# Chunked attention and a Fourier mixing block on one core: the first batch's fold halves joined in PSUM, sines ahead of the exponentials, Pool work re-ranked

## The chip, the cores and the metric

One NeuronCore of a Trainium2 chip runs the kernel. The metric is the device time of one execution in microseconds; below it is written "us". The engines are TensorE (PE, with PEld for its weight loads), VectorE (DVE), ScalarE (ACT), GpSimd (POOL) and SyncE (SP, which only issues transfers here).

## The reference, cut to what matters

There are 4 batches, 8 heads, 768 positions and 64 numbers per head. Each chunk of 32 positions attends to 8 memory keys and to its context of 16 positions to the left, itself and 8 to the right. The heads' outputs side by side are `x` (768 x 512 per batch).

```python
for c in range(24):
    k_full = concat([mem_k, k[l_start:r_end]]); v_full = concat([mem_v, v[l_start:r_end]])
    a = softmax(q_c @ k_full.T / 8)
    x[c] = a @ v_full
u = x + real(fft(fft(x, axis=1), axis=2))        # over positions, then over the 512 columns
un = (u - mean(u)) / sqrt(var(u) + 1e-6)
out = u + relu(un @ w_ch1) @ w_ch2               # 512 -> 2048 -> 512
```

## The kernel before, in words

The kernel has three parts per batch: attention for four pairs of heads, the Fourier step, and an MLP. It builds a list of tasks with an engine, a cost, predecessors, buffers that are taken and given, and a rank. `Plan.order` (L54) runs a clock over these costs and writes down the tasks in the order in which they would start; each engine then gets its instructions in this order and works through them strictly in it. The plan's clock sets only the order. On the chip an instruction waits by a semaphore for those that share data or a buffer with it, and for nothing else.

**Attention** (`attention`, L654; pair number `n` 0 to 3 is the first batch). SP loads `q` and `k` in float32 (`qf`, `kf`, three buffers each) and `v` with a column of ones (`va`, three buffers). The queries and keys are cast to bfloat16 (`e_cast_q` L293, `e_cast_k` L297), on DVE for the first batch and on POOL for the others; POOL also copies the part of `va` that overlaps the next chunk (`e_overlap` L301). TensorE transposes both (`trq`, `trk`), ACT evicts them (`qT` L314, `kTb` L335), and for each half `g` of the sequence TensorE makes scores (`sc` L346, one buffer), ACT the exponential (`e` L354), TensorE the product with the values (`xa` L367, one PSUM buffer), and DVE divides by the sum into `xsb` (L377, L378). Scores need the copy of the memory keys into `kTb` (L330).

**Fourier, later batches** (`part_of_later` L780). The columns and positions are folded on DVE (`zy`, `pq`, `ff`), so that cosines and sines act on half the length. Each folded tile is split into a float16 part `hi` (ACT, L425) and the remainder `lo` (DVE, L430). TensorE multiplies both with the tables `cosS`, `sinS` along positions (`ps`, L440: the row products), `up` holds the result as two float16 parts again (L452 on ACT, L456 on DVE), `dn` is its reversal (L461), and TensorE multiplies with the tables `cosD`, `nsinD`, `sinD` along columns (`pm`, L472).

**Fourier, first batch** (`part_of_first` L808). The folding is done by halves `h` of the column range, so that the half of pairs 0 and 1 (heads 0, 1, 6, 7) can start before pairs 2 and 3 are there: `pq` L482 and L483, `ff` L497 to L500. Each half has its own row products, cosine and sine, and its own `up`; one edge column gets twelve products with one column of weights (`e0_edge`, L509). The columns step then adds up eight products for each of the two parities of the output column, those of the second half with the tables `tab1` that POOL makes from `alt` (L739, L740): 16 products for each of six tiles, 96 in all (`pm` L531).

**Tail of a Fourier step**: for each of six tiles `kt`, DVE adds `pm` to `xsb` (L538), makes mean and variance (L544, L545), ACT subtracts the mean (`un` L550), TensorE transposes (`tp` L557), and DVE evicts into `unT` (L562). POOL makes `rstd` (L566).

**MLP** (`mlp` L882): `ph` (L578, 64 matmuls per half batch), relu on ACT (`hT` L585), `pc` (L592, 48), then `osb` on DVE (L598) and the store. POOL issues the loads of both weights, which are cast to float16 on the way: `w1` (L770) behind the last overlap copy of the first batch, `w2` (L775) behind those of the second pair of the second batch.

**The tables**: DVE makes angles in three steps (L636, L639, L641) and their absolute value (L644) for positions (`S`) and columns (`D`); the sines are one ACT task (`e_all_sines`, seven activations, L719 to L724) that depends on the last exponential of the first batch:

```python
t_sines = add("ACT", 6.2, e_all_sines, [t_angle["S"], t_angle["D"], x_last])
```

POOL then turns `tab1` and writes the tables' first rows (L747 to L752). Where no other task of TensorE is ready, the plan puts groups of six products with zeros (`warm` L390).

Of the kernel before, what the change touches and what calls it, by code (L numbers as in the profile page):

```python
# [12 lines left out]
FP16 = mybir.dt.float16  # L13
AFT = mybir.ActivationFunctionType
# [20 lines left out]
class Plan:  # L35
# [18 lines left out]
    def order(self):  # L54
        now, idle, wire = 0.0, {}, 0.0
# [8 lines left out]
        while any(waiting.values()):  # L64
# [4 lines left out]
            for e, ts_ in waiting.items():  # L69
                if idle.get(e, 0.0) > now:  # L70
                    continue
                for t in ts_:
# [17 lines left out]
                    if t["moved"]:  # L90
                        wire = max(wire, now + cost) + t["moved"]
                        t["done"] = t["end"] = wire + self.LAG["DMA"]
                    else:
                        t["done"] = now + cost + self.LAG.get(e, 0.07)
# [20 lines left out]
def kernel(  # L115
# [40 lines left out]
    NS = 3  # L156
    qf = [spool.tile([QP, 2, RB * D], FP32, name=f"qf{i}") for i in range(NS)]
# [6 lines left out]
    HP = H // 2  # L164
# [21 lines left out]
    svD = cpool.tile([P, 1], FP32)  # L186
    zero = cpool.tile([P, 1], FP32)
# [15 lines left out]
    tab1_of = []  # L203
    alt = wpool.tile([P, 2, HD], FP16)
    c384 = cpool.tile([P, NST], FP32)
    e256 = cpool.tile([P, 2, NST], FP16)
    w1_sb = wpool.tile([P, NDT, DFF], FP16)
    w2_sb = wpool.tile([P, NHT, DM], FP16)

    def e_zero():  # L210
        nc.vector.memset(zeros, 0.0)
        nc.vector.memset(zero, 0.0)  # L212
        nc.vector.memset(hpi_b, math.pi / 2.0)
        nc.vector.memset(mhalf, -0.5)

# [39 lines left out]
    def e_mkf():  # L255
        for par in range(2):
            nc.scalar.dma_start(mkf[:, par], bass.AP(
                tensor=mem_k.tensor, offset=mem_k.offset + par * NMEM * D,
                ap=[[2 * NMEM * D, NPR], [D, NMEM], [1, D]]))
# [12 lines left out]
    def e_load_v(n, hh):  # L272
        b, pr = seq[n]
        v1 = va[n % NV]
# [26 lines left out]
    def e_overlap(n, hh):  # L301
        v1 = va[n % NV][:, hh]
# [47 lines left out]
    def e_exp(n, g):  # L350
        sc = sc_of.pop((n, g))
        e1_of[n, g] = e1 = apool.tile([P, 2, 6, 64], FP32, tag="e1", bufs=3, name="e1")
# [5 lines left out]
    def e_values(n, g):  # L358
        e1 = e1_of.pop((n, g))
        xa = aps.tile([P, 3, 2, 66], FP32, tag="xa", bufs=1, name="xa")  # L360
        xa_of[n, g] = xa
        for st in range(3):
            for hh in range(2):
                v1 = va[n % NV][:, hh]
# [17 lines left out]

    warm_of = []
# [10 lines left out]
    mu_of, unT_of, rstd_of = {}, {}, {}  # L394

# [24 lines left out]
    def e_hi(b, par, ab):  # L420
        if ab == 0:
# [10 lines left out]

    def e_rows(b, par, ab):
        ps_of[b, par, ab] = ps = fps.tile([P, 2, NK], FP32, tag="acc", name="ps")

        def dft(out_, tab, c0, c1):
            for sp in range(2):
                for st in range(3):
                    for i, part in enumerate(hl_of[b, par]):
                        nc.tensor.matmul(out_[:, sp, :], part[:, ab, sp * 3 + st, c0:c1],  # L440
                                         tab[:, sp, st, :], start=(st == 0 and i == 0),
                                         stop=(st == 2 and i == 1))

        dft(ps, cosS if ab == 0 else sinS, 0, P)
        if par == 0 and ab == 1 and b > 0:
            dft(ps[0:1], cosS, 0, 1)
# [29 lines left out]

    def e0_pq(h, i):
# [8 lines left out]
        elif i == 1:  # L486
            nc.vector.tensor_copy(e256[:, 0], pq[:, :, P])
            nc.vector.tensor_tensor(e256[:, 1], pq[:, :, P], e256[:, 0], ALU.subtract)

    def e0_ff(h, ab):  # L490
# [4 lines left out]
        op = ALU.add if ab == 0 else ALU.subtract  # L495
        if h == 0:
            nc.vector.tensor_copy(ff[:, ab, :, 0], pq[:, :, 0])  # L497
        else:
            nc.vector.tensor_tensor(ff[:, ab, :, 0], pq[:, :, 0], c384, op)
        nc.vector.tensor_tensor(ff[:, ab, :, 1:P], pq[:, :, 1:P],  # L500
                                rev_ap(pq, HD - 1, P - 1, [[HD, NST]]), op)

    def e0_edge():

        ps_of["edge"] = ps = fps.tile([P, 2, NK], FP32, tag="acc", name="ps")
        for sp in range(2):
            for st in range(3):
                for i in range(2):
                    nc.tensor.matmul(ps[0:1, sp, :], e256[:, i, sp * 3 + st:sp * 3 + st + 1],  # L509
                                     cosS[:, sp, st, :], start=(st == 0 and i == 0),  # L510
                                     stop=(st == 2 and i == 1))

    def e0_edge_up(part):
        up = up_of[0, 0, 1][2][0:1]
        if part == 0:
            nc.scalar.copy(up[:, 0].rearrange("p k s -> p s k"), ps_of["edge"][0:1])
        else:
            nc.vector.tensor_tensor(up[:, 1].rearrange("p k s -> p s k"), ps_of.pop("edge")[0:1],
                                    up[:, 0].rearrange("p k s -> p s k"), ALU.subtract)

    def e0_columns(kt):
        pm_of[0, kt] = pm = fps.tile([P, 2, HD], FP32, tag="acc", name="pm")
        tab1 = tab1_of[0]
        for par in range(2):
            im = 0
            for h in range(2):
                for ab in range(2):
                    i = 0 if ab == 0 else (1 if kt < 3 else 2)
                    rhs = (cosD, nsinD, sinD)[i] if h == 0 else tab1[:, i]
                    for part in range(2):  # L530
                        nc.tensor.matmul(pm[:, par, :],  # L531
                                         up_of[0, h, ab][kt // 3][:, part, ts(kt % 3, P)],
                                         rhs[:, par, :], start=(im == 0), stop=(im == 7))
                        im += 1
# [12 lines left out]
    def e_un(b, kt):  # L547
        un_of[b, kt] = un = fpool.tile([P, DM], FP16, tag="un", bufs=3, name="un")

        nc.scalar.activation(un, xs[b][:, kt, :], AFT.Identity, bias=mu_of[b][:, kt, 0:1],  # L550
                             scale=-1.0)

    def e_turn_u(b, kt):
        un = un_of.pop((b, kt))
        tp_of[b, kt] = tp = fps.tile([P, NDT, P], FP16, tag="acc", name="tp")
# [3 lines left out]
    def e_unT(b, kt):  # L559
        if kt == 0:  # L560
            unT_of[b] = fpool.tile([P, NDT, S], FP16, tag="unT", bufs=2, name="unT")
        nc.vector.tensor_copy(unT_of[b][:, :, ts(kt, P)], tp_of.pop((b, kt)))  # L562
# [44 lines left out]
    t_mkf = add("ACT", 0.2, e_mkf, moved=0.8)  # L607
# [3 lines left out]
    t_clear["va", 0, 0] = add("ACT", 1.0, lambda: e_clear_act(va[0][:, 0]), [t_zero])  # L611
    t_clear["va", 0, 1] = add("POOL", 0.9, lambda: nc.gpsimd.memset(va[0][:, 1], 0.0))
    t_scales = add("DVE", 0.2, e_scales, [t_iota])
    t_idb = add("DVE", 0.25, lambda: nc.vector.tensor_copy(ident_b, ident), [t_id])
    t_masks = add("POOL", 0.9, e_masks)
    for i in range(1, NS):
        t_clear["kf", i] = add("ACT", 1.15, lambda i=i: e_clear_act(kf[i]), [t_zero])
        for hh in range(2):
            t_clear["va", i, hh] = add("ACT", 1.0, lambda i=i, hh=hh: e_clear_act(va[i][:, hh]),
                                       [t_zero])  # L620
    for i in range(NKT):
        t_clear["kTb", i] = add("POOL", 0.5, lambda i=i: nc.gpsimd.memset(
            kTb[i].rearrange("p (b c) -> p b c", b=NB)[:, :, 64:96], 0.0))
    t_col = add("DVE", 0.6, e_rows_of_ones, [t_id])
    t_ones = {i: add("DVE", 0.1, lambda i=i: e_ones(i),
                     [t_col, t_clear["va", i, 0], t_clear["va", i, 1]]) for i in range(NV)}
# [6 lines left out]
    for nm, parts, y, r, NN, c in (("S", tabS, yS.rearrange(fl3), rS.rearrange(fl3), S, 1.3),  # L633
# [328 lines left out]
```

## Time and profile before

| what | value |
|---|---|
| time, median of 7 runs | 319.54 us (317.72 to 323.25) |
| the profiled execution | 319.59 us, of which the span from first to last instruction is 317.8 us |
| mean granted TensorE clock | 0.984 of full speed |
| busy: PE, DVE, ACT, POOL | 295.2, 191.4, 167.9, 88.8 us |
| first exponential; last one of the first batch | starts 11.40; ends 32.7 us |
| the seven sines and their table load | 32.72 to 38.3 us |
| first product of the columns step; first MLP product | 54.7; 70.0 us |
| TensorE busy in 40 to 48 us | 3.34 us of 8, at clock 0.84 |

A line of the timeline or of the groups gives the start and length, or the count, busy time and mean length in ns, then engine, source line, operation, and "output<-input" by the program's names. A line of the chain of waits gives start, length, engine, tile and line. A busy TensorE is not TensorE at its peak, since matmuls overlap; the spacing of their starts is what one costs (84 ns for a row product, 109 for one of the columns, 163 for `ph`, 216 for `pc`).

### The profile page before, as it was taken

How to read it: one execution, taken by the hardware profiler on the slowest of the kernel's cores; microseconds unless marked ns; L12 is line 12 of the kernel's file. 1: busy time of each engine (PE TensorE's matmuls, PEld its weight loads, DVE VectorE, ACT ScalarE, POOL GpSimd, SP SyncE). 2: the span in 40 equal slices, each digit the busy share in tenths (PEclk: the TensorE clock that was granted, in tenths of full speed). 3: DMA queues.
4: the chain of work that ended last, by engine and by line, in shares of the span. 5: the costliest groups of instructions: out<-in, count | busy, mean ns of one | idle time of the engine just before them, and what ended most of it. 6: DMA issues, size and time to landing. Idle time of an engine off the chain costs nothing.

```text
span 317.8 us, 7416 instructions
## 1 busy us (share of the span) xinstructions
PE 295.2 (93%) x3099; PEld 195.0 (61%) x3099; DVE 191.4 (60%) x355; ACT 167.9 (53%) x298; POOL 88.8 (28%) x110
## 2 busy tenths in 40 slices
PE   6686849999999989999999999999999999999994
PEld 6575738886655657874767755676554454554641
DVE  7899798774229999879978789838600101002001
ACT  7765935658943767576486604743261270340710
POOL 5436696648416544248002020000100000000000
PEclk9999787999999999999999999999999999999999
DMA  6998999999506396911111001000100100101001
GB/s 178 202 189 203 212 241 203 192 207 204 123 33 185 89 218 159 196 35 57 68 28 29 2 35 67 2 0 33 52 16 35 67 0 35 66 0 66 35 33 66
DMA packets 41888, 30.68 MB, mean 97 GB/s; under 512 B 30080, under 2 KB 32128, under 8 KB 41856
## 3 DMA queue, kind: packets, MB, share of 16 engines
q1 hardware_dynamic: 35424, 19.67, 30.5%
q0 software_dynamic: 2688, 4.19, 7.5%
q10 hardware_dynamic: 3744, 6.36, 5.3%
q8 instruction: 24, 0.39, 0.6%
q14 instruction: 8, 0.07, 0.1%
HBM read 28.11 MB, written 6.29 MB: 108 GB/s over the span
## 4 chain that ended last, share of the span: by engine, by line
PE 74%; DVE 18%; ACT 2%; DMA 2%; SPq 1%; issue 1%; ACTq 0%
PE ph L578 25%; PE pc L592 23%; PE xa L367 7%; PE pm L472 5%; PE ps L440 5%; PE pm L531 3%; DVE pq L482 2%; DVE xsb L378 2%; DVE ff L417 2%; DMA qf<-in_q_dram 2%; PE sc L346 2%; PE tp L557 2%; DVE osb L598 2%; DVE zy L400 2%; PE trq L309 1%; DVE pq L407 1%
## 5 line engine op out<-in xcount | busy, mean ns | idle before, releaser
L578 PE MATMUL ph<-unT,w_sb 128*128 128x384 f16 x512 | 92.1, 326 | 2.2 <-DVE osb L598 1.1
L585 ACT ACTIVATE hT<-ph 128x384 f16<-128x384 f32 x128 | 61.2, 493 | 57.4 <-PE ph L578 55.9
L592 PE MATMUL pc<-w_sb,hT 128*128 128x512 f16 x384 | 88.5, 379 | 0.0
L578 PEld LDWEIGHTS <-w_sb 128*128 128x128 f16 x512 | 48.1, 97 | 36.3 <-issue 7.2
L598 DVE SCALAR_TENSOR_TENSOR osb<-pc,rstd,xsb 128x512 f32<-128x512 f32 x24 | 18.0, 748 | 78.2 <-PE pc L592 78.1
L592 PEld LDWEIGHTS <-hT 128*128 128x128 f16 x384 | 36.1, 98 | 39.2 <-issue 0.5
L303 POOL COPY va<-va 32x780 f32<-32x780 f32 x32 | 37.2, 1180 | 39.1 <-DMA va<-in_v_dram 29.4
L354 ACT ACTIVATE e<-sc,mbias 128x384 f32<-128x384 f32 x64 | 33.7, 579 | 18.7 <-PE sc L346 12.2
L367 PE MATMUL xa<-va,e 128*64 128x65 f32 x768 | 30.7, 229 | 6.9 <-POOL va L303 4.5
L367 PEld LDWEIGHTS xa<-va,e 128*64 128x64 f32 x768 | 26.0, 140 | 14.1 <-issue 5.7
L550 ACT ACTIVATE un<-xsb,mu_s 128x512 f16<-128x512 f32 x24 | 17.2, 722 | 24.1 <-DVE mu_s L545 15.7
L538 DVE TENSOR_TENSOR xsb<-pm,xsb 128x512 f32<-128x512 f32 x24 | 16.3, 678 | 9.2 <-PE pm L472 6.5
L425 ACT CAST hi<-ff 128x768 f16<-128x768 f32 x16 | 13.3, 833 | 15.6 <-DVE ff L417 9.3
L295 POOL CAST qb<-qf 96x1024 bf16<-96x1024 f32 x12 | 13.8, 1149 | 24.6 <-PE trq L309 17.6
L390 PE MATMUL warm<-zeros 128*128 128x128 bf16 x218 | 18.4, 241 | 1.0 <-DVE zero L212 1.0
L378 DVE TENSOR_TENSOR xsb<-xa,zs 128x384 f32<-128x384 f32 x32 | 17.8, 557 | 1.1
L299 POOL CAST kb<-kf 104x1024 bf16<-104x1024 f32 x12 | 14.0, 1168 | 13.7 <-issue 10.6
L566 POOL TENSOR_SCALAR rstd<-mu_s 128x6 f32<-128x6 f32 x4 | 1.7, 436 | 56.9 <-DVE osb L598 42.8
L544 DVE BATCH_NORM_STATS2 st<-xsb 128x6 f32<-128x512 f32 x24 | 16.6, 691 | 0.6
L430 DVE TENSOR_TENSOR lo<-ff,hi 128x768 f16<-128x768 f32 x16 | 16.3, 1035 | 0.8 <-ACT hi L425 0.8
L390 PEld LDWEIGHTS <-zeros 128*128 128x128 bf16 x218 | 14.9, 109 | 1.8 <-DVE zero L212 1.0
L452 ACT CAST up<-ps 128x386 f16<-128x386 f32 x16 | 9.7, 607 | 11.4 <-PE ps L440 8.6
(126 smaller groups left out, 390.3 us busy)
## 6 DMA issues: line engine op xcount, KB each, us to landing
qf<-in_q_dram SPq DMA_DIRECT2D x16, 384.0 KB
kf<-in_k_dram SPq DMA_DIRECT2D x16, 384.0 KB
out_dram<-osb ACTq DMA_DIRECT2D x24, 256.0 KB
va<-in_v_dram SPq DMA_DIRECT2D x32, 176.0 KB
w_sb<-in_moe_w_ch_dram POOLq DMA_DIRECT2D x8, 512.0 KB, 11.6
va<-in_mem_v_dram SPq DMA_DIRECT2D x32, 24.0 KB
va<-in_v_dram SPq DMA_DIRECT2D x16, 28.0 KB
va<-in_v_dram SPq DMA_DIRECT2D x16, 4.0 KB
```

What stands on the lines that cost most here:

```text
L303: nc.gpsimd.tensor_copy(v1[0:32, 1:NB, 0:D + 1], v1[96:128, 0:NT, 0:D + 1])
L354: nc.scalar.activation(e1[:, :, :, ts(half, 32)], sc[:, :, 0:6, ts(half, 32)], AFT.Exp, bias=mbias[:, half:half + 1], scale=1.0 / math.sqr ...
L367: nc.tensor.matmul(xa[64 * half:64 * half + 64, st, hh, 0:65], e1[:, hh, t6, :], v1[:, 6 * g + t6 + 1, 0:65], start=True, stop=True)
L378: nc.vector.tensor_tensor(xs[b][:, 3 * g:3 * g + 3, 2 * pr * D:(2 * pr + 2) * D] .rearrange("p s (h d) -> p s h d", h=2), xa[:, :, :, 0:D] ...
L390: nc.tensor.matmul(warm_of[0], zeros, zeros, start=True, stop=True)
L430: nc.vector.tensor_tensor(lo[:, ab].rearrange(fl), ff_of[b, par][:, ab].rearrange(fl), hi[:, ab].rearrange(fl), ALU.subtract)
L544: nc.vector.bn_stats(st6, xs[b][:, kt, :])
L550: nc.scalar.activation(un, xs[b][:, kt, :], AFT.Identity, bias=mu_of[b][:, kt, 0:1], scale=-1.0)
L578: nc.tensor.matmul(ph[:, 0:384], w1_sb[:, dt, ts(ht, P)], unT_of[b][:, dt, sh * 384:(sh + 1) * 384], start=(dt == 0), stop=(dt == NDT - 1))
L585: nc.scalar.activation(hT_of[b, sh][:, ht, :], ph_of.pop((b, sh, ht))[:, 0:384], AFT.Relu, bias=0.0, scale=-1.0)
L592: nc.tensor.matmul(pc_of[b, sh, stl], hT_of[b, sh][:, ht, ts(stl, P)], w2_sb[:, ht, :], start=(ht == 0), stop=(ht == NHT - 1))
L598: nc.vector.scalar_tensor_tensor(osb, pc_of.pop((b, sh, stl)), rstd_of[b][:, st:st + 1], xs[b][:, st, :], ALU.mult, ALU.add)
```

## The change

1. **Halves joined.** The row products of the first batch are made for parity `par` and kind `ab`, and both halves `h` add up in one PSUM tile; for the second half and `par != ab` the table is a negated copy (`neg`, two DVE instructions). So there are 96 row products instead of 48 and 24 products of one column instead of 12, but one `up` per (`par`, `ab`) as in the later batches, and 8 products instead of 16 for each tile of the columns. The four sums lie in two `acc`, one `mlp` and the `tr` buffer. `tab1`, `alt` and POOL's work on them are gone. The first half's `hi` and `lo` lie in the space of `hT`.
2. **Sines.** They are three tasks behind the angles, ahead of all exponentials; a first tiny sine brings its table at the start. The angle steps on DVE get a high rank, and their absolute value is taken with an integer operation. The loads of the memory keys move from ACT's queue to SP's.
3. **Clears.** POOL's clear of `va[0]` and ACT's of `va[2]` change places in part: ACT clears `va[0]`, `va[1]`; POOL clears `va[2]` and a fourth `va` that lies in the space of `w2` and serves pair 3; in the plan POOL's masks come after the S angles and its clears after the D angles. The clears in `kTb` go to DVE. The last exponential of the first batch also lies in `w2`'s space.
4. **Second PSUM buffer for `xa`**: pairs 2 and 3 use `tr` for `g = 1`.
5. **POOL's casts and overlap copies of the second batch** depend, in the plan, on the last `lo` of the first.
6. **Tail of the first batch**: the sum on DVE also gives the mean (`accum_out`), `un` follows it at once, the statistics come later in rank, and `unT` is evicted by ACT; its transposes use `mlp` for the first three tiles.
7. In the plan, transfers issued by POOL have a wire of their own for the time they land.

```diff
-                    if t["moved"]:
+                    if t["moved"] and e == "POOL":
+                        beside = max(beside, now + cost) + 1.15 * t["moved"]
+                        wire = max(wire, now + cost) + t["moved"]
+                        t["done"] = beside + self.LAG["DMA"]
+                        t["end"] = now + cost
+                    elif t["moved"]:
...
-            nc.scalar.dma_start(mkf[:, par], bass.AP(
+            nc.sync.dma_start(mkf[:, par], bass.AP(
...
+    def xtag(n, g):
+        return "tr" if n in (HP - 2, HP - 1) and g == 1 else "xa"
...
+    def row_products(out_, parts, ab, tab, c0, c1, first=True, last=True):
+        for sp in range(2):
+            for st in range(3):
+                for i, part in enumerate(parts):
+                    nc.tensor.matmul(out_[:, sp, :], part[:, ab, sp * 3 + st, c0:c1],
+                                     tab[:, sp, st, :], start=(first and sp + st + i == 0),
+                                     stop=(last and sp + st + i == 4))
...
+    def e0_rows(par, ab, h):
+        if h == 0:
+            pool, tag = ((fps, "acc"), (fps, "mlp"), (aps, "tr"))[0 if ab == 0 else 1 + par]
+            more = dict(bufs=1) if tag == "tr" else {}
+            ps_of[0, par, ab] = pool.tile([P, 2, NK], FP32, tag=tag, name="ps0", **more)
+        ps = ps_of[0, par, ab]
+        turned = h == 1 and par != ab
+        tab = neg_of[0][:, ab] if turned else (cosS if ab == 0 else sinS)
+        row_products(ps, hl_of[0, h], ab, tab, 0, P, h == 0, h == 1)
+
+    def e0_columns(kt, ab):
+
+        if ab == 0:
+            pm_of[0, kt] = fps.tile([P, 2, HD], FP32, tag="acc", name="pm")
         for par in range(2):
-            im = 0
-            for h in range(2):
-                for ab in range(2):
-                    i = 0 if ab == 0 else (1 if kt < 3 else 2)
-                    rhs = (cosD, nsinD, sinD)[i] if h == 0 else tab1[:, i]
-                    for part in range(2):
...
+            rhs = cosD if ab == 0 else (nsinD if kt < 3 else sinD)
+            for part in range(2):
+                nc.tensor.matmul(pm_of[0, kt][:, par, :],
+                                 up_of[0, par, ab][kt // 3][:, part, ts(kt % 3, P)],
+                                 rhs[:, par, :], start=(ab + par + part == 0),
+                                 stop=(ab + par + part == 3))
+
+    def e0_sum(kt):
...
+        nc.vector.scalar_tensor_tensor(uv, pm_of.pop((0, kt)), 1.0, uv, ALU.mult, ALU.add,
+                                       accum_out=mean[:, kt, 0:1])
+        nc.vector.tensor_scalar(mean[:, kt, 1:2], mean[:, kt, 0:1], 1.0 / DM, None, ALU.mult)
...
+    t_masks = add("POOL", 0.9, e_masks, [t_angle["S"]])
+    for i in range(2, NV + 1):
+        for hh in range(2):
+            t_clear["va", i, hh] = add("POOL", 0.9, lambda i=i, hh=hh: nc.gpsimd.memset(
+                va[i][:, hh], 0.0), [t_angle["D"]])
...
+    t_sines = []
+    for i, nm in enumerate("SSD"):
+        t_sines.append(add("ACT", (1.35, 1.35, 1.8)[i], lambda i=i: e_sines(i), [t_angle[nm]]))
+    t_rows = add("POOL", 1.9, e_table_rows, [t_sines[2]], rank=125)
+    t_neg = [add("DVE", 0.4, lambda i=i: e_neg(i), t_sines[:2], rank=140 + i,
+                 take=("unT",) if i == 0 else ()) for i in range(2)]
...
+        calm = kept["f0"] if b == 1 else None
...
-        cq = add(cn, cc, lambda: e_cast_q(n, ce), [lq], take=("qb",), give=("qf",), margin=mgl)
-        ck = add(cn, cc, lambda: e_cast_k(n, ce), [lk], take=("kb",), give=("kf",), margin=mgl)
-        ov = [add("POOL", 0.84, lambda hh=hh: e_overlap(n, hh), [lv[hh]], margin=mgl) for hh in range(2)]
+        cq = add(cn, cc, lambda: e_cast_q(n, ce), [lq, calm], take=("qb",), give=("qf",), margin=mgl)
+        ck = add(cn, cc, lambda: e_cast_k(n, ce), [lk, calm], take=("kb",), give=("kf",), margin=mgl)
+        ov = [add("POOL", 0.84, lambda hh=hh: e_overlap(n, hh), [lv[hh], calm], margin=mgl) for hh in range(2)]
...
-            x_ = add("ACT", 1.16 if (n, g) != (HP, 0) else 2.44, lambda g=g: e_exp(n, g), [s_, t_masks] + (kept["f0"] if b == 1 else []), take=("e1",),
+            x_ = add("ACT", 2.44 if (n, g) == (0, 0) else 1.16, lambda g=g: e_exp(n, g),
+                     [s_, t_masks] + (t_sines if (n, g) == (0, 0) else [kept["x"]]), take=("e1",) if (n, g) != (HP - 1, 1) else (),
...
-    t_sines = add("ACT", 6.2, e_all_sines, [t_angle["S"], t_angle["D"], x_last])
...
+        kept["f0"] = lo
...
+            un = add("ACT", 0.72, lambda kt=kt: e_un(b, kt), [sa if b else su], take=("un",))
...
+            t_un[kt] = add("DVE" if b else "ACT", 0.43 if b else 0.6, lambda kt=kt: e_unT(b, kt), [tp, t_un.get(kt - 1)],
```

## The prediction, made before the changed kernel was run

> **What bounds the kernel now.** I read the page first, then the chain of waits in order of time, then the timeline of its first 70 us, then the busy time by stretches. The slices say that TensorE is full from about 55 us on: before that its share falls to 4 tenths, and the granted clock falls with it.
>
> ```profile
> PE   6686849999999989999999999999999999999994
> ...
> PEclk9999787999999999999999999999999999999999
> ```
>
> From the first MLP product to the end (70.0 to 317.8 us, 247.8 us) TensorE stands idle for about 8 us. So the time is the moment at which the first product `ph` starts, plus the TensorE work still open then. The chain shows how that moment comes about (start, length, engine, tile and line):
>
> ```profile
> 39.32 4.30 DVE pq L482
> ...
> 46.63 2.10 PE ps L509 x12
> ...
> 50.12 1.94 PE ps L440 x12
> ...
> 54.93 5.24 PE pm L531 x48
> ...
> 70.21 1.30 PE ph L578 x8
> ```
>
> A fold sum that takes 0.57 us elsewhere (34.81 us) takes 4.30 us at 39.32; two row products run at half pace (160 ns a matmul, 84 ns at 52.9 us); the columns' 96 matmuls fill TensorE together with attention of the second batch. The timeline shows why the fold sum was slow, and an earlier case of the same:
>
> ```profile
> 3.54 1.98 DVE L636 TENSOR_SCALAR yS<-tri,svS 128x386 f32<-128x386 f32 x1
> 3.63 0.84 POOL L622 MEMSET kTb<- 128x416 bf16 x2
> ...
> 5.05 0.25 POOL L730 MEMSET alt<- 128x128 f16 x1
> ...
> 39.03 1.04 POOL L295 CAST qb<-qf 96x1024 bf16<-96x1024 f32 x1 [2.75 <-issue]
> ...
> 43.17 0.97 POOL L740 TENSOR_TENSOR tab<-cosD,alt 128x256 f16<-128x256 f16 x1
> ```
>
> In both places Pool has a row of instructions back to back, and the DVE instruction (0.42 and 0.57 us undisturbed) ends only when that row does. The Trainium skill, page "SBUF — State Buffer", section "Who interferes with whom", says that Pool and DVE share a port pair as an exclusive lock, held for one instruction: DVE would then lose at most one Pool instruction, about 1 us. The row differs: it lost 3.7 us to a run of six. I use the row for runs, the rule for single instructions.
>
> **The start, 0 to 20 us.** The plan puts Pool's masks after the S angles, Pool's four clears after the D angles, and the second batch's casts after the last `lo`. But a semaphore comes only with shared data. In the built program masks and clears have no wait for DVE, and the second batch's first cast waits for its load, the previous cast and the transposes only. Both holds are thus order on paper. After `ident` (2.03 us) Pool does the masks (0.8) and four clears at 0.82 (row of L612), to 6.2 us; DVE's identity cast and the first three angle steps stand till then. From there, by the spacing of the rows: cast 0.2, three steps 0.39, 0.72, three steps 0.58, and the integer absolute value at 0.75 (row of L639, same size; 1.35 if it runs like the old L644): S angles at 10.8. By the one-instruction rule: 8.5. D angles +1.8 = 12.6. Sines (rows at 34.02 to 37.57 us): four of S 2.5 us to 13.3, three of D 1.75 to 15.1.
>
> Only now come DVE's casts of the first two pairs, the mask copies and the clears of `kTb` moved from Pool: 3.8 us from the rows, and 1.3 us for Pool's `va` copies and eight row memsets between, 17.7. Scores of pair 0 stand in TensorE's order behind the transposes of pair 1: 18.7. Then the table load and the exponential: 20.2, against 11.40 us before. So moving the sines first costs 8.8 us here. Of three table loads at 1.28 us (at 2.04, 32.72, 55.24) two are left, and the second is still in the path here. Memory keys move from ACT's queue to SP, two issues of 0.65 us ahead of `va`; `va` of pair 0 waits for its ones (7.6) anyway, lands near 13.5, needed after 21: nothing.
>
> **20 to 37 us.** ACT in its new order: seven exponentials at 1.05, three key and two query copies at 0.85 and 0.80, and some 2.3 us of waits for the single score buffer with a warm group ahead: 34.0. Two `hi` at 0.83, the last exponential 35.7 to 36.8 (31.65 to 32.7 before). Middle sines and their load, 32.72 to 38.3, are gone. Loads don't hold this: pair 3's values in `w2`'s space free them from a buffer, but the DMA share was full (1.16, 1.10 in 8 to 24 us) and they landed by 28.35; the exponentials are later. Their overlap copies end near 29.5.
>
> **37 to 51 us.** The second bank for `xa` makes the last four follow one another: the last ends at 38.3, is normalised by 39.5. Four fold sums at 0.56, plus 1.0 for Pool (casts and `va` copies at 32 to 42, no table products any more): 42.5. Edge parts (four tiny rows, 0.17 at most each) 43.0; two `ff` at 0.92, `hi` 0.83, two `lo` at 0.95, `kTb` copy 0.27: second `lo` 47.1. Row products: 24 at 84 ns on the first `lo` to 47.8, 24 on the second to 49.8; `up` 0.6, rest 0.6: 51.2. The first half's 48 (4.0 us) lie behind the last `xa`, under the fold sums; the edge's 24 (12 before, 2.0 us) under `ff` and `lo`. Were that cover gone: +2.0 each. The negated tables (two DVE rows of 0.4 to 0.75) fall before the third pair's casts: nothing. TensorE's pauses are short here (0.7 us before the last 48), so I take full clock; at the old 160 ns it costs 3.6 us more.
>
> **51 to the first MLP product.** Columns halve: 48 matmuls at 109 ns, 5.2 us, against 96. Sum with accumulate 0.75 (row of L598, the nearest; 0.69 by L538), mean 0.1, `un` 0.72, transposes 0.4, `unT` on ACT 0.6 (0.41 on DVE before). Statistics (0.87 a tile) leave this way. ACT sets it: four `un`, three `unT`, one query copy, 5.5 us after the first sum at 52.3, with TensorE's own 7.0 us beside it: first `ph` at 58.4. Before 70.0: 11.6 us earlier. `w1` is issued by 32 and took at most 16.7 us to land: in time. `w2` is issued behind casts that wait for pair 4's transposes, 55.5 to 58.5; needed 71.8 to 78; landing 8.2 to 16.7: just in time.
>
> **What is owed.** At its first `ph` the old kernel had done for the second batch three query and three key transposes, four scores, two `xa`, and one `tp` more; the new one has one of each transpose. Owed: 2 x 0.35 + 2 x 0.46 + 4 x 0.28 + 2 x 0.85 + 0.22 = 4.7 us. In the first sixteen `ph` groups ACT has 16 relus at 0.49 and 5.5 us of `un`, `unT`, exponential and copies, 13.4, as much as TensorE; with two buffers I count 1.0 us of stall. Net: 11.6 - 4.7 - 1.0 = 5.9 us. The profiled execution took 319.59 us (span 317.8; the median of the runs is 319.54): 313.7 us.
>
> **Rivals.** (a) *The port costs little*: Pool and DVE alternate, as at 97.6 to 101 us where two sums took 1.67 and 1.58. Angles at 8.5, 2.3 us earlier, and 1.3 us less twice: 308.8. For it: those rows; against: 3.54 and 39.32 us. Chance 0.14.
> (b) *The first exponential is too late*: at 12 to 20 us Pool has four `va` copies (pairs took 3.78 and 2.71 us, up to 6.5) and eight memsets (1.3), 7.8 us, of which I count 1.3. If DVE stands for all of it, as at 39.32, the exponential starts at 26.7, and all behind it moves by 6.5; TensorE, idle since its warm-up, then runs the first `xa` at the slow rate (1.57 for 0.85, twice, 1.4 us): 321.6, slower. It decides past 26.1 us for the first exponential. Against: those copies wait for loads, so they come one by one. Chance 0.19, with other slips of that size.
> (c) *Given back in the second batch's Fourier*: its attention now starts with the MLP, and between its last `xa` and its first row products the new order has 11.2 us of TensorE work, where the old kernel took 13.9 (94.8 to 108.7). Lost once 2.7, in both halves 5: 316.4 to 318.7, take 318.5. Chance 0.12, mostly within 0.5%.
> The forecast itself (312 to 317) has 0.55.
>
> **Range and chances.** 0.5% is 1.6 us, about what a measurement of this kernel tells from no change. Faster 0.73, same 0.08, slower 0.19. Range 308 to 322: from (a) to (b), with the clock's 3.6 us and the 2.0 of the edge inside.
>
> **What would show it.** First exponential near 20 us; yS and the casts beside Pool's clears ending at 6.2; the second batch's first Pool cast near 32 us, not after the last `lo`; second `lo` at 47; columns start near 50; first `ph` at 58 with `pm` at 5.2 us in all; second batch's first `xa` only after that. The forecast is wrong if the first `ph` is not before 64, or if TensorE idles over 14 us behind it.

## The result and the profile after

| | before | after |
|---|---|---|
| time, median | 319.87 us (64 runs) | 315.59 us (27 runs) |
| profiled execution, span | 319.59, 317.8 us | 316.41, 314.5 us |
| first exponential | 11.40 | 19.44 |
| first product of the columns step | 54.7 | 49.2 |
| first MLP product `ph` | 70.04 | 57.55 |
| from there to the end | 247.8 | 256.9 |
| of it TensorE idle | 7.8 | 9.4 |

The ratio is 0.9879, 95% interval 0.9863 to 0.9896: 3.9 us faster; 5.9 was forecast. Of every view only the lines that matter are shown here. The slices of the changed kernel's page:

```profile
PE   8389899999998979999999999999999999999994
...
PEclk9689999999999998999999999999999999999999
```

TensorE reaches 9 tenths in the 4th slice instead of the 7th, but it dips in the 13th and the 15th (94 to 102 and 110 to 118 us; the kernel before has only an 8 in the 15th), and the clock is lower in the 16th. The chain of waits shows both the earlier start and the dips (start, length, engine, tile and line):

```profile
37.92 4.15 PE ps L466 x48
45.29 4.04 PE ps L466 x48
49.33 0.87 PE pm L567 x8
57.55 1.46 PE ph L630 x8
96.60 2.69 DVE pq L434
104.70 3.42 DVE lo L459 x2
115.34 1.73 PE ph L630 x8
117.50 2.05 PE ps L466 x12
```

Up to 57.55 it runs as the prediction wrote it: 48 row products on each half, at 84 ns, six tiles of columns (8 products each), then the MLP. Behind it stand two long pieces of DVE, in the second batch's fold, and twelve row products that took 2.05 us instead of 1.01 (their starts are 160 ns apart instead of 84).

What was predicted for the start is in the timeline: Pool's clears beside DVE's casts and angles, and the second batch's first casts ahead of the last `lo`:

```profile
2.81 1.57 POOL L701 MEMSET va<- 128x858 f32 x2
...
3.00 3.82 DVE L683 TENSOR_SCALAR yS<-tri,svS 128x386 f32<-128x386 f32 x3
4.30 1.57 POOL L701 MEMSET w_sb<- 128x858 f32 x2
...
36.18 1.54 POOL L313 CAST qb<-qf 96x1024 bf16<-96x1024 f32 x1
...
45.17 0.94 DVE L459 TENSOR_TENSOR lo<-ff,hi 128x768 f16<-128x768 f32 x1
```

The clears end at 5.87, and three angle steps (0.42 each undisturbed) end just behind them. The hold of Pool's work is not there.

**The balance.** The first `ph` came 12.5 us earlier. From it to the end 9.2 us were added: TensorE has 5.9 us more of work, 1.6 more of idle time, and 1.7 lost to the clock (0.79 of full speed over 112 to 120 us). 12.5 - 9.2 = 3.3 us, the difference of the two spans. The question of the experiments is thus twofold: what makes `ph` early, and what gives 3.3 us back behind it.

### The profile page after: what moved, and what is told of

Its sections match the earlier page's. It is cut to its first block, busy times and chain, and to the rows that moved or that the text cites. A ratio compares the mean times of both kernels' runs of the same rounds, so it can differ in the third digit from the quotient of the medians.

```text
span 314.5 us, 7515 instructions
## 1 busy us (share of the span) xinstructions
PE 296.1 (94%) x3147; PEld 196.3 (62%) x3147; DVE 187.3 (60%) x367; ACT 168.4 (54%) x302; POOL 79.6 (25%) x97
## 4 chain that ended last, share of the span: by engine, by line
PE 71%; DVE 19%; DMA 5%; ACT 3%; issue 2%; POOL 0%; ACTq 0%; DVEq 0%
PE pc L644 23%; PE ph L630 20%; PE ps L466 8%; PE xa L389 6%; PE pm L501 5%; DMA w_sb<-in_moe_w_ch_dram 5%; DVE pq L434 2%; DVE zy L426 2%; PE sc L364 2%; PE pm L567 2%; DVE ff L443 2%; DVE osb L650 2%; PE tp L606 2%; PE warm L415 2%; DVE xsb L400 1%
## 5 line engine op out<-in xcount | busy, mean ns | idle before, releaser
L637 ACT ACTIVATE hT<-ph 128x384 f16<-128x384 f32 x128 | 61.4, 493 | 60.5 <-PE ph L630 59.1
L321 POOL COPY va<-va 32x780 f32<-32x780 f32 x30 | 28.9, 971 | 57.6 <-DMA va<-in_v_dram 51.9
L376 ACT ACTIVATE e<-sc,mbias 128x384 f32<-128x384 f32 x62 | 32.7, 580 | 14.8 <-PE sc L364 12.4
L389 PE MATMUL xa<-va,e 128*64 128x65 f32 x720 | 27.5, 226 | 1.4 <-DVE xsb L400 1.4
L389 PEld LDWEIGHTS xa<-va,e 128*64 128x64 f32 x720 | 23.5, 138 | 6.3 <-issue 4.8
L597 ACT ACTIVATE un<-xsb,mu_s 128x512 f16<-128x512 f32 x18 | 12.9, 720 | 19.9 <-DVE mu_s L591 12.8
L415 PE MATMUL warm<-zeros 128*128 128x128 bf16 x254 | 19.2, 235 | 1.0 <-DVE zero L227 1.0
L454 ACT CAST hi<-ff 128x768 f16<-128x768 f32 x14 | 11.6, 831 | 13.0 <-DVE ff L547 6.4
L399 DVE RECIPROCAL zs<-xa 128x6 f32<-128x6 f32 x32 | 6.0, 189 | 20.3 <-PE xa L389 20.2
L415 PEld LDWEIGHTS <-zeros 128*128 128x128 bf16 x254 | 16.7, 107 | 1.5 <-DVE zero L227 1.0
L332 ACT COPY qT<-trq 128x768 bf16<-128x768 bf16 x16 | 12.8, 800 | 6.3 <-PE trq L327 4.5
L618 POOL TENSOR_SCALAR rstd<-mu_s 128x6 f32<-128x6 f32 x4 | 1.6, 390 | 56.9 <-DVE mu_s L591 56.7
```

What stands on the lines that cost most here:

```text
L321: nc.gpsimd.tensor_copy(v1[0:32, 1:NB, 0:D + 1], v1[96:128, 0:NT, 0:D + 1])
L376: nc.scalar.activation(e1[:, :, :, ts(half, 32)], sc[:, :, 0:6, ts(half, 32)], AFT.Exp, bias=mbias[:, half:half + 1], scale=1.0 / math.sqr ...
L389: nc.tensor.matmul(xa[64 * half:64 * half + 64, st, hh, 0:65], e1[:, hh, t6, :], v1[:, 6 * g + t6 + 1, 0:65], start=True, stop=True)
L415: nc.tensor.matmul(warm_of[0], zeros, zeros, start=True, stop=True)
L637: nc.scalar.activation(hT_of[b, sh][:, ht, :], ph_of.pop((b, sh, ht))[:, 0:384], AFT.Relu, bias=0.0, scale=-1.0)
```

## The experiments

All were edited from the changed kernel, but for before_casts, and have 4 to 10 runs each. "Rest" is the time from the first `ph` to the end; "idle" TensorE's idle time in it (some 4.1 us of it at the very end in every run); "clock" what a granted clock below full speed cost there, by stretches of 4 us (each counted whole, with the idle time in it; this matters in margin_27 alone). Where a price in us is given for a run, it is the difference of its ratio to that of the changed kernel, times 319.87.

| run | first `ph` | rest | idle | clock | time | ratio to before |
|---|---|---|---|---|---|---|
| before | 70.0 | 247.8 | 7.8 | 0 | 319.87 | 1 |
| changed kernel | 57.6 | 256.9 | 9.4 | 1.7 | 315.59 | 0.9879 [0.9863, 0.9896] |
| sines_last | 64.2 | 253.5 | 8.2 | 0 | 320.95 | 1.0057 [1.0026, 1.0088] |
| angles_last | 64.3 | 254.9 | 9.5 | 0 | 320.61 | 1.0023 [0.9987, 1.006] |
| columns_twice | 63.9 | 254.1 | 8.5 | 0 | 318.86 | 0.9991 [0.9962, 1.0021] |
| tail_old | 64.1 | 254.6 | 8.3 | 1.7 | 319.92 | 1.0002 [0.9963, 1.0041] |
| xa_single | 60.2 | 253.3 | 7.9 | 0 | 316.46 | 0.9908 [0.9872, 0.9944] |
| clears_held | 61.5 | 254.5 | 8.7 | 0 | 317.75 | 0.9962 [0.9922, 1.0002] |
| pool_held | 59.1 | 256.3 | 8.8 | 1.7 | 314.85 | 0.9878 [0.981, 0.9946] |
| rows_late | 57.7 | 256.6 | 9.3 | 1.7 | 315.94 | 0.987 [0.982, 0.992] |
| casts_act | 57.7 | 252.4 | 7.1 | 0 | 311.46 | 0.9735 [0.9682, 0.9788] |
| held_rows_acts | 57.5 | 252.2 | 7.0 | 0 | 311.87 | 0.9766 [0.9725, 0.9808] |
| margin_27 | 57.7 | 278.1 | 24.2 | 10.2 | 336.44 | 1.0523 [1.0469, 1.0576] |
| before_casts | 68.1 | 248.2 | 8.1 | 0 | 319.5 | 0.9992 [0.9958, 1.0025] |

First, the parts that make `ph` early.

**sines_last.** The sines behind the first batch's last exponential.

```diff
-    t_first = add("ACT", 1.4, e_first_sine, [t_zero])
-  [s_, t_masks] + (t_sines if (n, g) == (0, 0) else [kept["x"]])
+  [s_, t_masks] + ([] if (n, g) == (0, 0) else [kept["x"]])
     x_last = [attention(n) for n in range(HP)][-1]
+    for t in t_sines: t["after"].append(x_last)
-  hi = add("ACT", 0.85, lambda ...: e_hi(0, h, ab), [ff, hi],
+  hi = add("ACT", 0.85, lambda ...: e_hi(0, h, ab), [ff, hi] + t_sines,
```

> The changed kernel, with the sines behind the first batch's last exponential again (the early table load is left out, the first `hi` waits for the sines because its buffer is theirs). My account: first exponential near 11 us instead of 19.4, but 6 us of sines and two more table loads (1.28 each) stand behind the last exponential, so the first half's row products start near 41 instead of 37.9 and the first MLP product near 59.5 instead of 57.6; time 317.5, +1.5 to +2.5 on 315.6. Rival, the late first exponential is what the change pays for: the whole row moves up, first MLP product near 55, time 313. Rival, the placing of the sines is all of the gain: 319.5.

Measured: the direction of my account, but at more than twice its size, 1.8% of the time or 5.7 us; the second rival (319.5) was nearer. Lines of its timeline, then of its chain of waits:

```profile
40.15 1.57 ACT L454 CAST hl<-ff 128x768 f16<-128x768 f32 x2
40.80 1.14 POOL L313 CAST qb<-qf 96x1024 bf16<-96x1024 f32 x1
40.97 1.06 DVE L522 TENSOR_TENSOR both<-pq,c 128x6 f32<-128x6 f32 x2
...
43.21 1.82 DVE L459 TENSOR_TENSOR hl<-ff,hl 128x768 f16<-128x768 f32 x2
```

```profile
44.22 11.73 PE ps L466 x119
```

The first `hi` waits for the sines until 40.15, the first half's `lo` come from 43.2 on, and all 120 row products (119 in the record) stand in one row from 44 to 56 us. In the changed kernel the first half's 48 and the edge's 24 were done by then, under the fold sums and `ff`. That is the cover that the prediction priced at 4.0 and 2.0 us, against the 6.6 us by which `ph` is late. But 2.2 us of this delay are not the sines' own: from 40.97 to 43.2 DVE makes the edge parts beside two casts of Pool (1.06 and 0.90 us instead of 0.23 and 0.17), and only then the `lo`. So the run prices the lost cover together with that. The first exponential hardly moved (18.50 for 19.44; I had expected 11), which left open what makes it late.

**angles_last.** As before, and the angles on DVE with their old ranks (100, 110, 120, 130) behind the casts.

> The run with the sines behind the last exponential showed the first exponential at 18.5, not near 11: the angles still stood ahead of the casts on DVE. Here the angles have their old places behind the casts as well, so that all of the order of the start is undone. My account (the angles on DVE, not the sines on ACT, make the first exponential late, and the sines behind the exponentials cost more than that): first exponential near 11 to 13, last exponential near 32, but the row products still wait for sines and the first `hi`, first MLP product 62 to 64, time 319.5 to 321, no better than with the sines alone moved. Rival, the late start is what costs: first MLP product near 57, time 314 to 315.5.

Measured: `ph` (64.3) and time as in sines_last, as my account had it. The first exponential came at 15.71 (11 to 13 expected), 2.8 us earlier than in sines_last, but the last one is no earlier than in the changed kernel (35.38 to 36.4; 32 expected). So here the late first exponential costs nothing, since the row behind it has slack. The slack is limited: in pool_held and columns_twice, where the first exponential is 2.6 to 2.7 us later than in the changed kernel, the last one is 1.3 to 1.5 us later.

**columns_twice.** Each of the first batch's column products issued twice, which doubles that batch's Fourier sum.

```diff
-  for part in range(2):
+  for j, part in enumerate((0, 0, 1, 1)):
```

> The changed kernel with each of the first batch's 48 column products issued twice (the first batch's Fourier sum is doubled, so its output changes). This puts the 5.2 us of TensorE work back that the joining of the halves took out. My account, TensorE full from the first MLP product on: first MLP product 5.2 us later (62.7), time 320.8. Rival, what comes early is given back anyway in the second batch's Fourier, whose chain on DVE sets the time there: first MLP product 5.2 us later, but the idle in 93 to 121 us shrinks, time 317 to 318.

Measured: 1.1% slower than the changed kernel, 3.6 us, for 5.2 us of work put back. In the two profiles `ph` came 6.4 us later (some of it from the start, see pool_held) and the rest was 2.8 us shorter: idle 0.9 less, no slow clock (1.7). Both accounts hold in part: TensorE's work counts, and part of what comes early is given back in the second batch.

**tail_old.** `un` behind the statistics, which get their old rank, and `unT` on DVE.

```diff
-  un = add("ACT", 0.72, ..., [sa if b else su], ...)
+  un = add("ACT", 0.72, ..., [sa], ...)
-  t_un[kt] = add("DVE" if b else "ACT", ...)
+  t_un[kt] = add("DVE", ...)
```

> The changed kernel, with the first batch's tail as before the change: `un` waits for the statistics (0.87 us a tile on DVE) instead of the accumulated mean, and `unT` is copied by DVE instead of ACT. My account: the statistics stand between sum and `un` and DVE carries sums, statistics and copies, so the first MLP product comes 1.5 to 2.5 us later, near 59.5 (61 where the start is the late one), time 317 to 317.5. Rival, TensorE's columns set the tail: first MLP product within 0.5 us, time 315.6.

Measured: `ph` 6.5 us later (1.5 to 2.5 expected), time 3.9 us more. The timeline shows that the statistics aren't the main thing:

```profile
58.75 0.52 PE L327 MATMUL trq<-ident_b,qb 96*128 96x96 bf16 x8 [1.88 <-POOL qb L313]
...
63.67 0.54 PE L343 MATMUL trk<-ident_b,kb 104*128 104x104 bf16 x8 [2.92 <-POOL kb L317]
64.05 0.81 PE L630 MATMUL ph<-unT,w_sb 128*128 128x384 f16 x4
```

In the planned order transposes of the second batch now stand ahead of the first `ph`, and TensorE waits for Pool's casts, which stand behind the four `w2` issues (3.0 us from 59.54). So this run doesn't price the tail alone: a small change of costs moved two instructions in TensorE's queue.

**xa_single.** `xtag` returns "xa" always.

> The changed kernel with one bank for all `xa`, instead of a second one for the last halves of the first batch's last two pairs. My account: the last two or three `xa` wait for the norms, 0.6 to 0.8 us each, so the fold sums, and the first MLP product, come 1 to 1.5 us later; time 316.8. Rival, the second bank does nothing (the exponentials set the pace, 1.5 us apart): 315.6.

Measured: the last two `xa` start at 39.35 and 41.65 instead of 35.37 and 37.00, `ph` is 2.7 us later, and the time 0.9 us more, with overlapping intervals. The rest is 3.7 us shorter: again an early `ph` is worth less than its earliness.

Now Pool's places at the start.

**clears_held.** A one-element Pool copy that reads the D angles ahead of `e_masks`, and the masks planned behind the D angles.

> The changed kernel, with a one-element Pool copy that reads the D angles ahead of the masks and the four clears, so that the planned order holds on the chip. My account (Pool's row of clears stops DVE): S angles end near 7 instead of 10, first exponential near 16.5 instead of 19.4, last exponential and first MLP product 2 us earlier, time 313.5. Rival, the start is set by ACT and loads: first exponential within 0.7 us of 19.4, time 315.6. Rival, the clears now meet the casts of the first pairs: first exponential later, 317.

Measured: slower than the changed kernel by 0.8% (2.7 us), as the second rival had it. The angles were quick (D done at 9.5 instead of 12.24), but the clears then met the casts:

```profile
11.44 1.57 POOL L702 MEMSET va<- 128x858 f32 x2
11.49 3.15 DVE L349 COPY kTb<-mkT 128x96 bf16<-128x96 bf16 x1
12.94 1.57 POOL L702 MEMSET w_sb<- 128x858 f32 x2
```

A copy that takes 0.28 us takes 3.15, until the four clears are through. The first exponential gained 0.7 us (18.75), but the second came at 23.84 (21.59 in the changed kernel) and all behind it late. Pool's row of clears stops DVE wherever it stands; beside the angles this is cheaper.

**pool_held.** The hold of the second batch's Pool work made real.

```diff
         kept["f0"] = lo
+        kept["hold"] = add("POOL", 0.1, lambda: nc.gpsimd.tensor_copy(
+            sv0, hl_of[0, 1][1][:, 1, 0, 0:1]), [lo])
-        calm = kept["f0"] if b == 1 else None
+        calm = kept["hold"] if b == 1 else None
```

> The changed kernel, with a one-element Pool copy that reads the first batch's last `lo` ahead of the second batch's first cast: the hold that the plan asks for, made real. My account (the hold was never there, and not needed, since the fold sums at 39 to 41 us ran at 0.55 already): first cast near 46.5 instead of 36.2, first MLP product unchanged at 57.5, the weights w2 issued some 5 to 10 us later, so that the second MLP products wait for them: 318 to 322. Rival, Pool beside DVE costs the first batch's chain: first MLP product 1 to 2 us earlier, time 314.

Measured: no difference clear of the noise, so my expectation failed on the time. The first cast came at 47.09, but the one that the `w2` issues stand behind waits for transposes at 56.7 anyway, and the issues were no later (58.63; 60.32 in the changed kernel). The hold is neither there nor needed.

This run and columns_twice have, instruction for instruction, the start of the changed kernel, and yet the first exponential at 22.17 and 21.99 instead of 19.44. The timeline of pool_held:

```profile
11.51 1.93 POOL L321 COPY va<-va 32x780 f32<-32x780 f32 x2 [5.64 <-DMA va<-in_v_dram]
...
13.39 0.28 POOL L721 MEMSET nsinD<- 1x128 f16 x1
13.40 1.89 DVE L313 CAST qb<-qf 96x1024 bf16<-96x1024 f32 x1
```

Pool's copies began 1.1 us earlier than in the changed kernel, as soon as the values had landed, so the copies and the eight memsets (until 14.74) made one row, and DVE's cast (0.68 alone) ended only behind it, at 15.29. That is the mechanism of the prediction's rival (b), at 2.7 us instead of 6.5. In columns_twice the copies began 0.9 us earlier, with the same effect. That the landing decides which of the two starts an execution gets is read from these profiles; no run sets it.

**rows_late.** The eight memsets behind the first batch's last overlap copies.

```diff
     x_last = [attention(n) for n in range(HP)][-1]
+    t_rows["after"].append(x_last)
```

> The changed kernel, with Pool's eight row memsets (nsinD, sinD) behind the first batch's last value copies and the w1 issues instead of among the start. Two runs whose start is instruction for instruction that of the changed kernel had the first exponential at 22.0 and 22.2 us, not 19.4: Pool's value copies and these memsets stood in one row, and a DVE cast of 0.68 us took 1.89. My account (a Pool row stops DVE): without the memsets the row is shorter, first exponential 19 to 20.5 in this profile, first MLP product at 57 to 58, time 314.5, 1 us under the changed kernel. Rival, the value copies alone stop DVE, or loads set the start: first exponential at 22, time 315.6.

Measured: the first exponential at 19.27 and the last of the first batch at 34.07 to 35.1, 1.3 us earlier, but `ph` at 57.69 and no gain.

```profile
37.69 1.04 POOL L313 CAST qb<-qf 96x1024 bf16<-96x1024 f32 x1
37.73 1.44 DVE L512 TENSOR_TENSOR pq<-xsb 128x384 f32<-128x384 f32 x1
38.67 1.40 POOL L317 CAST kb<-kf 104x1024 bf16<-104x1024 f32 x1
39.10 1.39 DVE L513 TENSOR_TENSOR pq<-xsb 128x384 f32<-128x384 f32 x1
```

The earlier fold sums now run beside the second batch's casts, 1.4 us instead of 0.55. The first of them ends at 39.17, behind the first cast and well before the second one ends (40.07): between two casts that follow at once DVE does get in.

Last, what gives back behind `ph`.

**casts_act.** The third batch's casts on ACT instead of Pool.

```diff
         ce, cn, cc = (nc.vector, "DVE", 0.68) if first else (nc.gpsimd, "POOL", 1.04)
+        if b == 2:
+            ce, cn, cc = nc.scalar, "ACT", 0.9
...
```

In the plan each cast of the third and fourth batch also comes behind the one before it.

> The changed kernel, with the third batch's casts of q and k on ACT instead of Pool (with them each cast after the one before it, in the third and fourth batch). My account of what was given back (DVE's chain in the second batch's Fourier, slowed by Pool beside it): the fold difference of 2.77 us at 96.5 falls to 0.95 to 1.3, the two `lo` of 3.49 to 1.9, TensorE's idle time in 93 to 121 us from 3.5 to below 1.5, time 313.5. Rival, ACT's order sets it (a relu behind a `hi` that waits for DVE): four casts more on ACT make it worse, 316 to 318.

Measured: 0.9735, 4.6 us less than the changed kernel. The stretch of the second batch's Fourier in the timeline of the changed kernel:

```profile
95.65 1.84 POOL L313 CAST qb<-qf 96x1024 bf16<-96x1024 f32 x1 [7.12 <-DMA qf<-in_q_dram]
96.51 2.77 DVE L434 TENSOR_TENSOR pq<-zy 128x768 f32<-128x768 f32 x1
...
104.50 1.10 POOL L313 CAST qb<-qf 96x1024 bf16<-96x1024 f32 x1 [1.48 <-DMA qf<-in_q_dram]
104.63 3.49 DVE L459 TENSOR_TENSOR lo<-ff,hi 128x768 f16<-128x768 f32 x2
...
115.34 1.73 PE L630 MATMUL ph<-unT,w_sb 128*128 128x384 f16 x8 [1.97 <-ACT hT L637]
```

and of casts_act:

```profile
97.55 1.59 DVE L434 TENSOR_TENSOR pq<-zy 128x768 f32<-128x768 f32 x1
...
104.06 0.95 DVE L459 TENSOR_TENSOR lo<-ff,hi 128x768 f16<-128x768 f32 x1
...
105.05 0.95 DVE L459 TENSOR_TENSOR lo<-ff,hi 128x768 f16<-128x768 f32 x1
```

The busy time in 93 to 121 us (stretch, its length, then busy PE, PEld, DVE, ACT and POOL with their counts, clock, DMA share, GB/s), of the changed kernel:

```profile
93.00:121.00 28.00, 24.52 (x347) 17.47 (x346) 27.12 (x40) 19.45 (x36) 12.76 (x12) 0.94 1.01 195
```

and of casts_act:

```profile
93.00:121.00 28.00, 27.02 (x351) 18.34 (x350) 21.95 (x37) 23.39 (x42) 8.64 (x7) 1.00 0.64 120
```

DVE falls from 27.1 busy of 28 us to 22.0, TensorE's idle time from 3.5 to 1.0, and the clock stays full. From the `zy` at 94.64 to the batch's last `lo` it took 24.0 us; in casts_act, from 95.68, it took 20.4. ACT took four casts more without harm, and its order still has relus behind a `hi`: DVE's lateness is the cause, and ACT's order passes it on. The DMA share fell too, 1.01 to 0.64, but it is not what slows DVE: both quick `lo` of casts_act ran at a share of 1.20 and 1.14 (101 to 105 and 105 to 109 us).

**margin_27.** `SPARE[1]` from (1.5, 0.7, 2.0) to (1.5, 2.7, 2.0).

> The changed kernel, planned with 2.7 us instead of 0.7 of spare time for the second batch's work on ACT and DVE, so that the relus stand ahead of the `hi` casts that wait for DVE. If ACT's order makes the pause of 2 us at 113 to 115 (and the slow clock behind it): the pause goes, the granted clock stays full at 112 to 120, time 313.5. If DVE's chain is the bound and ACT's order only shows it: TensorE waits elsewhere, for the row products, time 315.6 within 0.8.

Measured: 1.0523; neither account. The margin holds for every ACT and DVE step of the second batch, its attention too: its `xa` start 4.2 to 5.5 us apart from 75 to 109 us (2.3 to 4.8, from 70 to 95, in the changed kernel), its first `lo` at 121.5 instead of 104.6, and TensorE ran out of work. So this says nothing about ACT's order.

**before_casts.** The same move of the third batch's casts, made in the kernel before.

> The kernel before, with the third batch's casts of q and k on ACT instead of Pool (each cast after the one before it in the third and fourth batch). If Pool beside DVE in the second batch's Fourier is a price that the changed order brought (its third batch's loads and casts fall into that stretch): the old kernel gains little, 0 to 1.5 us of its idle 2.3 us in 102 to 118, time 318.5 to 319.5. If it is a price that both pay: 4 us as in the changed kernel, time 315.5.

Measured: no gain, 0.9992, and a rest of 248.2 against 247.8. The old kernel's DVE was nearly as full (26.4 us of 28 in 94 to 122 us, with fold sums of 1.58 and 1.67 us), so Pool slows DVE in both orders. But the move did not relieve DVE here as it did in casts_act: Pool's copies of `va` took the place of the casts beside the fold,

```profile
104.40 3.10 DVE L430 TENSOR_TENSOR lo<-ff,hi 128x768 f16<-128x768 f32 x2
```

DVE was still busy for 25.4 us, its way from `zy` to the last `lo` took 23.9 us instead of 24.7, and TensorE's idle time in the stretch was 2.7 us, not less than the 2.3 before. So the run doesn't show that the old order would hide a slow DVE.

**held_rows_acts.** The edits of rows_late, pool_held and casts_act at once.

> Three edits on the changed kernel at once: the row memsets late, the second batch's first casts really held behind the last `lo` (a one-element Pool copy that reads it), and the third batch's casts on ACT. With the rows late alone the first exponential came at 19.3, but the second batch's casts then met the fold sums (1.44 and 1.39 us instead of 0.55) and took the gain back. My account: with the hold those sums run at 0.55, second `lo` ends near 44.5 instead of 46.1, first MLP product 56 to 56.5, and the stretch of the second batch as with the casts on ACT: time 310, about 1.5 under that run. Rival, the first MLP product is set by something else again: 311.5.

Measured: 0.9766, no better than casts_act alone. The fold sums ran at 0.55 and the second `lo` ended at 45.2 (46.1), but the columns started at 49.12 (49.17) and `ph` came at 57.5. TensorE's own lines show what sets it:

```profile
44.40 0.84 PE L415 MATMUL warm<-zeros 128*128 128x128 bf16 x12
45.08 0.25 PE L466 MATMUL ps<-cosS,hi 128*128 128x193 f16 x1
```

The first `lo` of the second half was there at 44.22, but twelve zero products stand ahead in TensorE's order, and from the first half's products at 37.80 (37.85 in the changed kernel) to the columns the order runs as before. An earlier `lo` gains nothing there.

## Why the prediction was right, and where it was off

**Start, right in its steps.** Pool's clears to 6.2 (5.87), S angles 10.8 (10.1), D angles 12.6 (12.24), sines to 15.1 (13.85), first exponential 20.2 (19.44, or 22.0 and 22.2 in two runs with the same start). The choice between the row and the rule set these numbers, though the first exponential turned out to matter little (angles_last). The Trainium skill ("SBUF — State Buffer", section "Who interferes with whom") has the lock held for one instruction; by that the S angles end at 8.5. They ended at 10.1 in the changed kernel, and in clears_held a 0.28 us copy waited through four clears. But "ends only when that row does" is too strong for every row. The sum at 39.32 in the kernel before ended at 43.62, behind six of Pool's instructions, while a seventh (43.17 to 44.14) and four memsets followed without a pause; and in rows_late a sum got in between two casts, as the page's rule has it. DVE stood for the whole row beside the clears and beside the eight memsets; what makes the difference isn't shown. Beside a single copy of 1.36 us it lost 0.64 us (`pq` 1.59 instead of 0.95 in casts_act).

**The middle, right.** Last exponential 35.7 to 36.8 (35.34 to 36.4), fold sums to 42.5 (41.2), second `lo` 47.1 (46.1), second half of the row products 45.8 to 49.8 (45.13 to 49.17), columns 5.2 us in all, `ph` at 58.4 (57.55). "Not there" was right for the hold of Pool's casts, which began at 36.18. The cover of 4.0 and 2.0 us fits sines_last, with the reserve made there.

**Owed, too small: 4.7 us, measured 5.9.** The groups behind `ph` count two `xa`, four scores and two query transposes more than before, as predicted, and one and a half key transposes instead of two. Priced by spacing they are 4.5 us; TensorE's busy time at full clock grew by 5.9, and the other 1.4 us are not explained.

**The mis-sized term: "with two buffers I count 1.0 us of stall".** It was 3.3 us more than before, 1.6 idle and 1.7 by the clock behind a pause of 2 us. I had placed it at ACT in the first sixteen `ph` groups, where TensorE was full to 72 us. It came 40 us later, as in rival (c), which I gave 0.12: the part of the second batch's fold that counts there begins at 94.64 (96.59 before), hardly earlier, since its attention starts with the MLP now, and Pool slows DVE in it. With DVE relieved the loss is gone (casts_act).

Why the old order loses less there is not shown. Its TensorE had 40 products of `ph` and 28 of `pc` in 94 to 122 us; the new one has 56 of `ph` and none of `pc` in 93 to 121. Each `ph` group has a relu to wait for, on an ACT whose `hi` waits for DVE, while `pc` groups follow one another. That this makes the difference is read from the two timelines; no run isolates it.

The clock's 1.7 us are not a fixed price of the pause either. The same wait stands in clears_held, and in columns_twice with 1.89 us, and the clock stayed full behind it:

```profile
118.35 1.46 PE L631 MATMUL ph<-unT,w_sb 128*128 128x384 f16 x8 [1.97 <-ACT hT L638]
```

**The sum.** 12.5 - 5.9 - 3.3 = 3.3 us in the profiles, 3.9 by the ratio of the runs (the profiled execution of the changed kernel lies 0.8 us above its median). Against the forecast's 5.9 the start of `ph` was better by 0.9, the owed work worse by 1.2 and the stall worse by 2.3: in part the errors cancel, which is luck. That the time lies in the range, 308 to 322 us, says little, since the unchanged time lies in it too; the times of the single steps are the better evidence.

**What is not settled.** The parts don't add up: undone singly, the sines cost 5.7, the columns 3.6 and the tail 3.9 us, more than the whole gain. Each `ph` later by 6 us made the rest 2 to 3.5 us shorter, and tail_old's price is one of queue order. The statistics' own price wasn't isolated. The hold of Pool's work is not there on the chip (36.18), and made real it changed nothing clear of the noise (pool_held).

## What to carry to other kernels

An earlier start of the full stretch is worth only what the next bottleneck leaves of it: add up TensorE's work, its idle time and its clock behind that point, and look at the next stage whose chain is on another engine. An order in a plan holds on the chip only where data or a buffer stands behind it; ask what instruction would wait. Before work is moved to Pool, look at what DVE does at that time: a row of Pool's instructions can stop DVE for the whole row (three angle steps took 3.82 us beside four clears), and ACT may be the better place, as for the casts here. Measure it in the order that will run: the same move gained nothing in the kernel before.

## What the runs showed that was not expected

The same program start ran in two ways (first exponential 19.44, or 21.99 and 22.17); in the late one Pool's copies of the values began 0.9 to 1.1 us earlier. A row of eight memsets of one row each (0.15 us apart) held a DVE cast for 1.2 us. A pause of 2 us of TensorE at 113.4 to 115.3 us was followed by row products 160 instead of 84 ns apart (clock 0.79 in 112 to 120 us); the same pause in clears_held (116.4 to 118.4 us) was not: the clock was full in 116 to 124 us.
